# Windowed attention and a routed two-layer MLP on one core: second weights loaded by expert and only when missing, and the small tiled matmuls of a unit issued in one block

## Chip, cores, metric

The kernel runs on one core of a Trainium2 chip. The metric is the device time of one execution in microseconds (us). Executions of one kernel scatter by about 1% either way here, so kernels are compared by runs that were interleaved on one chip: a ratio below is the mean time of one kernel's fast runs over the mean of the other's fast runs of the same rounds, so it is not quite the ratio of the medians that stand beside it. A run is called slow when it is over 1.5% above the fastest run of the same kernel; slow runs are left out of the ratios.

## The reference, cut to what matters

```python
# attention: 8 batches x 8 heads, 576 positions, head size 64, causal window of 64
scores = scale * q @ k.T, masked to 0 <= i - j < 64
x = softmax(scores) @ v                       # -> (8, 576, 512), heads side by side
# one expert of 8 per batch
e = argmax(mean(x, axis=1) @ w_gate)          # per batch
out = softmax_weight * (relu(x @ w1[e]) @ w2[e])   # w1: 512x1024, w2: 1024x512
```

With the fixed inputs, the experts of the eight batches are 5 4 2 7 1 5 7 2: five different ones, and the last three batches repeat earlier ones.

## The kernel before

A batch is worked in five slots: four head pairs and one slot for the last 64 positions. In slot `s` the kernel does the values step of unit `s-1` (`st_a`, PSUM tile `av`, normalised by DVE into `x`), the scores of unit `s` (`st_s`, tile `sp`), the transposes of q and k for unit `s+2` (`tr`, tile `tp`, 8 and 10 of them), and the transposes of `x` of unit `s-2` (`st_x`, tile `xps`). `fill(part)` puts expert work of an earlier batch in between: first matmuls (`ph`, 4 matmuls a chunk) and second matmuls (`po`, 8 a chunk). The values, scores and q/k transposes use half of the PE array each (tiled modes); expert matmuls and most transposes of `x` use all of it.

```python
wp  = tc.tile_pool(name="wp", bufs=3)      # expert weights w1t, w2t
op_ = tc.tile_pool(name="op", bufs=4)      # output tiles ob
ps  = tc.tile_pool(name="ps", bufs=6, space=PSUM)   # av, tp, xps, ph, po, gl, glp in turn
...
def norm(u, av, n, x):                     # frees an av buffer
    nc.vector.reciprocal(out=rl, in_=avv[:, :, D:D + 1])
    nc.vector.tensor_tensor(out=x, in0=avv[:, :, 0:D], in1=rl, op=ALU.mult)
...
def gate(b):
    # gl = pooled @ w_gate on PE; then gs, gm (max), gi (index) on DVE
    nc.gpsimd.load(ereg, gi[0:1, 0:1])                       # index into a register
    nc.gpsimd.dma_start(out=w1t, in_=w1e[esl].squeeze(0))    # 2 MB read, 1 MB written as fp16
    nc.gpsimd.dma_start(out=w2t, in_=w2e[esl].squeeze(0))
    # nm, ge (exp on ACT), gr
...
for s in range(NSLOT + 4):
    st_a(s - 1, 0); st_a(s - 1, 1)
    fill(0.1)
    mask_it = st_s(s)
    fill(0.3)
    tr(n, 0)
    mask_it()
    fill(0.5)
    st_x(s - 2)
    fill(0.75)
    tr(n, 1)
    cast_v(n); load_qk(n + 5); load_v(n + 3)
    fill(1.0)
    if s >= 7 and (s - 7) % NU == 0: gate((s - 7) // NU)
    if s >= 8 and (s - 8) % NU == 0: gate2((s - 8) // NU)
# then the expert work that is left
```

The softmax here doesn't subtract the row's maximum and nothing guards it: scores larger than these inputs give would overflow.

## Time and profile before

| kernel before | |
|---|---|
| median of the first 6 runs | 247.73 us (246.2 to 249.53) |
| profiled span | 246.9 us |
| start until the first expert matmul | 51.9 us |
| one batch in the middle (five slots) | 26.10 us |
| last batch's first expert matmul to the end | 21.2 us |

The page's slices of the kernel before; each digit is the busy share of one fortieth of the span, in tenths, and PEclk is the granted TensorE clock:

```profile
PE   0458876659999999999999999999999999998992
PEclk9999996559999999999999999999999999999999
DMA  6999999999499999999999999994993099479723
```

From 51.9 us on PE is idle only once, for 0.73 us, before its last matmuls are done. (The clock record begins only at 32.5 us here, and before its first entry the views print full clock. That is no measurement: in after_again, below, it begins at 55.1 us, and the first expert matmuls before that start 0.24 us apart, those after it 0.12 us. So the start ran at half clock there too.) The windows view gives the busy time of each engine between the starts of successive batches' first expert matmuls (third column: PE; the DMA share adds up the times of packets that overlap, so it can exceed 1):

```profile
core 0: us, PE busy (x) PEld busy (x) DVE busy (x) ACT busy (x) POOL busy (x), PEclk, DMA share, GB/s
79.93:106.03 26.10, 26.10 (x355) 15.92 (x351) 19.32 (x56) 15.20 (x38) 12.61 (x23) 1.00 1.11 219
184.33:207.09 22.76, 22.76 (x270) 13.85 (x266) 15.20 (x46) 11.68 (x30) 1.49 (x2) 1.00 0.58 122
207.09:225.69 18.60, 17.87 (x121) 10.55 (x118) 6.86 (x18) 6.15 (x17) 1.48 (x2) 1.00 0.75 155
225.69:246.87 21.18, 16.77 (x104) 10.12 (x104) 6.32 (x10) 4.94 (x12) 0.00 (x0) 1.00 0.52 141
```

PE is busy for all of the 26.10 us, so a gain there must come out of PE's own time. The timeline of PE in the middle shows where some of it is lost (start, duration of the merged group, line, tile; matmuls overlap, so the start-to-start difference is the cost):

```profile
113.56 1.16 PE L286 MATMUL ph<-xT,w1t 128*128 128x288 f16 x8
114.55 0.39 PE L228 MATMUL xps<-ident,x 128*128 128x128 f16 x4
114.77 0.65 PE L286 MATMUL ph<-xT,w1t 128*128 128x288 f16 x4
115.36 0.47 PE L147 MATMUL tp<-ident,qk 128*64 128x128 f16 x10
115.76 1.16 PE L286 MATMUL ph<-xT,w1t 128*128 128x288 f16 x8
116.84 0.35 PE L243 MATMUL gl<-wg,pl 128*1 128x8 f32 x8
```

Eight expert matmuls followed by the same mode (`128*128`) take 0.99 us, followed by another mode 1.08: about 0.1 us at each change. There are some 15 such changes out of expert work in a batch.

Last, the end: the last gate's matmul, its w1 load, and the first matmul that needs it. PE waits only 0.73 us for the load, since it still has the second matmuls of the batch before to do:

```profile
214.36 0.35 PE L243 MATMUL gl<-wg,pl 128*1 128x8 f32 x8
216.34 0.74 POOL L259 DMA_DIRECT2D w1t<-in_moe_w_dram  x1 [17.12 <-DVE gr L267]
225.69 0.54 PE L286 MATMUL ph<-xT,w1t 128*128 128x288 f16 x3 [0.73 <-DMA w1t<-in_moe_w_dram]
```

### The profile page before, as it was taken

What the parts mean: (1) busy time and instruction counts of PE and PEld (TensorE: products, weight loads), DVE (VectorE), ACT (ScalarE), POOL (GpSimd) and SP (SyncE); (2) the same over time, 40 slices, a digit from 0 to 9 for tenths busy, and PEclk for the clock granted to TensorE, in tenths of its full rate; (3) what the DMA queues carried; (4) which work ended last, traced back from release to release, by engine and by line L of the source; (5) the groups of instructions that cost most, each with busy time, mean ns of one, the idle gap of its engine ahead of it and who ended that gap; (6) DMA issues with size and microseconds to landing.
All of it is one profiled execution on the core that took longest, in us unless ns stands there. A gap on an engine that the chain in (4) does not pass through costs nothing.

```text
span 246.9 us, 7106 instructions
## 1 busy us (share of the span) xinstructions
PE 218.8 (89%) x2800; PEld 137.1 (56%) x2800; DVE 158.4 (64%) x460; ACT 125.2 (51%) x289; POOL 106.0 (43%) x191
## 2 busy tenths in 40 slices
PE   0458876659999999999999999999999999998992
PEld 0346555436655675566556665666556755745741
DVE  3467898807677767787768776886777564343232
ACT  2256667526734774377527753666357723602500
POOL 7987998942293139424772459022800110020000
PEclk9999996559999999999999999999999999999999
DMA  6999999999499999999999999994993099479723
GB/s 126 197 212 193 202 186 197 175 205 202 92 160 223 198 302 162 215 200 302 167 210 202 286 179 196 209 292 95 178 255 102 4 165 259 110 111 243 181 94 97
DMA packets 61489, 45.57 MB, mean 185 GB/s; under 512 B 40464, under 2 KB 48656, under 8 KB 61456
## 3 DMA queue, kind: packets, MB, share of 16 engines
q0 software_dynamic: 17664, 26.22, 62.7%
q1 hardware_dynamic: 43792, 18.90, 32.1%
q8 instruction: 22, 0.36, 0.6%
q14 instruction: 11, 0.09, 0.1%
HBM read 61.88 MB, written 9.44 MB: 289 GB/s over the span
## 4 chain that ended last, share of the span: by engine, by line
PE 73%; DMA 13%; POOL 6%; SPq 3%; issue 3%; DVE 1%; POOLq 0%; ACT 0%
PE ph L286 29%; PE po L301 25%; DMA w1t<-in_moe_w_dram 8%; PE tp L147 6%; DMA v_126<-in_v_dram 5%; PE sp L167 4%; PE av L202 3%; PE xps L228 3%; SPq L76 2%; POOL qk L65 2%; PE av L211 1%; PE gl L243 1%; PE glp L272 1%; POOL vx_149 L133 1%; POOL vxt_161 L137 0%
## 5 line engine op out<-in xcount | busy, mean ns | idle before, releaser
L286 PE MATMUL ph<-xT,w1t 128*128 128x288 f16 x512 | 77.1, 291 | 4.6 <-DMA w1t<-in_moe_w_dram 4.6
L301 PE MATMUL po<-w2t,hT 128*128 128x512 f16 (+1 forms) x320 | 74.9, 380 | 0.0
L286 PEld LDWEIGHTS <-w1t 128*128 128x128 f16 x512 | 44.9, 99 | 18.9 <-DMA w1t<-in_moe_w_dram 5.2
L174 ACT ACTIVATE pt<-sp 128x1024 f16<-128x1024 f32 (+1 forms) x40 | 37.6, 939 | 27.3 <-PE sp L167 27.0
L305 DVE TENSOR_SCALAR ob<-po,gw 128x512 f32<-128x512 f32 (+1 forms) x40 | 30.0, 749 | 30.3 <-PE po L301 27.7
L291 ACT ACTIVATE hT<-ph 128x288 f16<-128x288 f32 x96 | 37.6, 413 | 21.7 <-PE ph L286 20.0
L301 PEld LDWEIGHTS <-hT 128*128 128x128 f16 (+1 forms) x320 | 29.9, 100 | 31.1 <-issue 0.8
L147 PE MATMUL tp<-ident,qk 128*64 128x128 f16 x576 | 32.0, 249 | 10.7 <-DMA qk<-in_k_dram 10.7
L186 DVE TENSOR_TENSOR x<-av,rl 128x256 f16<-128x256 f32 (+1 forms) x80 | 33.8, 423 | 2.7
L147 PEld LDWEIGHTS <-qk 128*64 128x64 f16 x576 | 21.2, 125 | 20.6 <-issue 15.6
L259 POOL DMA_DIRECT2D w1t<-in_moe_w_dram x8 | 6.0, 755 | 56.4 <-DVE rl L185 38.8
L230 ACT ACTIVATE xT<-xps 128x512 f16<-128x512 f16 x32 | 19.2, 601 | 19.3 <-PE xps L228 19.3
L65 POOL DMA_DIRECT2D qk<-in_q_dram x32 | 19.7, 614 | 20.2 <-PE av L202 12.6
L177 DVE TENSOR_TENSOR pt<-pt,mask 128x1024 f16<-128x1024 f16 (+1 forms) x40 | 25.5, 637 | 0.7 <-ACT pt L174 0.6
L293 DVE TENSOR_SCALAR hT<-ph 128x288 f16<-128x288 f32 x32 | 14.5, 452 | 14.0 <-PE ph L286 14.0
L65 POOL DMA_DIRECT2D qk<-in_k_dram x32 | 19.5, 608 | 0.0
L202 PEld LDWEIGHTS <-pt 128*64 128x64 f16 x512 | 12.1, 120 | 9.9 <-DVE pt L177 8.1
L228 PE MATMUL xps<-ident,x 128*128 128x128 f16 (+1 forms) x160 | 16.1, 227 | 0.0
L228 PEld LDWEIGHTS <-x 128*128 128x128 f16 (+1 forms) x160 | 10.8, 102 | 8.4 <-issue 3.6
L185 DVE RECIPROCAL rl<-av 128x4 f32<-128x4 f32 (+1 forms) x80 | 13.6, 170 | 1.1 <-PE av L211 1.0
L153 ACT COPY kT_131<-tp 128x256 f16<-128x256 f16 (+1 forms) x12 | 5.5, 456 | 9.2 <-DVE qT_133 L152 9.0
L152 DVE COPY qT_148<-tp 128x256 f16<-128x256 f16 (+1 forms) x10 | 4.6, 463 | 8.5 <-PE tp L147 8.5
(211 smaller groups left out, 225.8 us busy)
## 6 DMA issues: line engine op xcount, KB each, us to landing
w1t<-in_moe_w_dram POOLq DMA_DIRECT2D x8, 1024.0 KB, 8.8
w2t<-in_moe_w_dram POOLq DMA_DIRECT2D x8, 1024.0 KB, 15.1
out_dram<-ob SPq DMA_DIRECT2D x32, 256.0 KB, 7.8
qk<-in_q_dram POOLq DMA_DIRECT2D x32, 144.0 KB, 6.8
qk<-in_k_dram POOLq DMA_DIRECT2D x32, 144.0 KB, 7.0
out_dram<-ob SPq DMA_DIRECT2D x8, 128.0 KB, 7.1
v_99<-in_v_dram SPq DMA_DIRECT2D x2, 128.0 KB, 3.0
v_110<-in_v_dram SPq DMA_DIRECT2D x2, 128.0 KB, 6.7
```

The costliest lines, as they stand in the source:

```text
L65: nc.gpsimd.dma_start(out=t[64 * i:64 * i + 64].rearrange("p h t d -> p h (t d)"), in_=src[b, 2 * hp:2 * hp + 2, :, :].rearrange("h (p t) ...
L147: nc.tensor.transpose(out=tp[64 * hh:64 * hh + 64, t].rearrange("p a b -> p (a b)"), in_=qks[n][:, hh, lo + t, :], identity=ident)
L174: nc.scalar.activation(out=pv, in_=sp[:, :, 0:64 * m], func=AF.Exp, scale=scale)
L177: nc.vector.tensor_tensor(out=pv, in0=pv, in1=mk.unsqueeze(1).broadcast_to([128, 2, 64 * m]), op=ALU.mult)
L186: nc.vector.tensor_tensor(out=x.rearrange("p (g d) -> p g d", d=D), in0=avv[:, :, 0:D], in1=rl[0:n].broadcast_to([n, 4, D]), op=ALU.mult)
L202: nc.tensor.matmul(out=av[64 * jj:64 * jj + 64, o:o + D + 1], lhsT=pt[:, hh, 2 * i + jj, :], rhs=vx[:, 1 - jj, i, hh, :], start=True, stop ...
L228: nc.tensor.transpose(out=tp[:, g], in_=x[0:n, g, :], identity=ident[0:n, 0:n])
L230: nc.scalar.activation(out=xTs[b][:, c, 0:512], in_=tp.rearrange("p g t -> p (g t)"), func=AF.Copy, accum_out=pps[b][:, c:c + 1])
L286: nc.tensor.matmul(out=ph[:, 0:SC], lhsT=w1v[:, kb, ft // 2, ft % 2, :], rhs=xTs[b][:, kb, ts(sc, SC)], start=(kb == 0), stop=(kb == NHP - 1))
L291: nc.scalar.activation(out=dst, in_=ph[:, 0:SC], func=AF.Relu)
L301: nc.tensor.matmul(out=po[0:n], lhsT=st["h"][:, ft, 128 * i:128 * i + n], rhs=w2t[:, ft // 2, ft % 2, :], start=(ft == 0), stop=(ft == 7))
L305: nc.vector.tensor_scalar(out=ob[0:n], in0=po[0:n], scalar1=gws[b][0:n, 0:1], scalar2=None, op0=ALU.mult)
```

## The change

Two ideas. All eight experts' second weights get a place of their own in SBUF (`WT`), so that an expert that comes again need not be loaded again; DVE keeps a vector of experts already seen and POOL issues the w2 load under the condition that this one is new. The second matmuls then address `WT` through a register. And the three tiled steps of a slot are put next to each other, with two fills instead of five, so that PE changes its mode less often.

```diff
-    wp = ctx.enter_context(tc.tile_pool(name="wp", bufs=3))
+    wp = ctx.enter_context(tc.tile_pool(name="wp", bufs=2))
+    WT = const.tile([128, E, 8 * Dm], FP16)
 def gate(b):
+        nc.vector.tensor_copy(out=gf, in_=gi[:, 0:1])
+        nc.vector.tensor_scalar(out=oh, in0=iota, scalar1=gf, ..., op0=ALU.is_equal)
+        nc.vector.tensor_tensor(out=st2, in0=oh, in1=seen, op=ALU.mult)
+        nc.vector.tensor_tensor(out=seen, in0=seen, in1=oh, op=ALU.max)
+        nc.vector.reduce_sum(out=gf, in_=st2, axis=AX.X)
+        nc.vector.tensor_copy(out=ei[:, 0:1], in_=gi[:, 0:1])
+        nc.vector.tensor_copy(out=ei[:, 1:2], in_=gf)
-        nc.gpsimd.load(ereg, gi[0:1, 0:1])
+        nc.gpsimd.load(ereg, ei[0:1, 0:1])
+        nc.gpsimd.load(hreg, ei[0:1, 1:2])
         nc.gpsimd.dma_start(out=w1t, in_=w1e[...])
-        nc.gpsimd.dma_start(out=w2t, in_=w2e[...])
+        nc.gpsimd.dma_start(out=WT[expert e], in_=w2e[...], cond=have < 1)
 # h_chunk, first of a batch
+        nc.tensor.load(pe, eis[b][0:1, 0:1])
 # o_chunk
-        rhs=w2t[:, ft // 2, ft % 2, :]
+        rhs=WT[:, ds(st["e"], 1), :]...[:, ft, :]
 # slot
             st_a(s - 1, 0); st_a(s - 1, 1)
-            fill(0.1)
             mask_it = st_s(s)
-            fill(0.3)
             tr(n, 0)
+            tr(n, 1)
             mask_it()
-            fill(0.5)
+            fill(0.3)
             st_x(s - 2)
-            fill(0.75)
-            tr(n, 1)
             cast_v(n); ...
             fill(1.0)
# ... cut: dependency declarations, and three loads moved up in the prologue
```

More of the change, by code (lines that the diff above doesn't have):

```diff
@@ L15 @@
 AX = mybir.AxisListType
+SYNC = mybir.DependencyInfo(mybir.DependencyClass.Sync, mybir.DependencyReason.DATA)
 @with_exitstack
@@ L54 @@
     qks, v32s, v8s, xTs = {}, {}, {}, {}
-    pts, xs, wts, gws, pps = {}, {}, {}, {}, {}
+    pts, xs, wts, gws, pps, eis, w1s = {}, {}, {}, {}, {}, {}, {}
     NP = B * NHP
@@ L82, in load_v @@
             nc.sync.dma_start(out=t8[64:128], in_=v[b, :, 512:576, :].rearrange("h p d -> p h d"))
+    WT = const.tile([128, E, 8 * Dm], FP16)
+    loads, tmms = [], []
     ident = const.tile([128, 128], FP16)
@@ L100 @@
     load_v(2)
+    load_qk(3)
+    load_v(3)
+    load_qk(4)
     wg = const.tile([128, NHP, E], FP32)
     nc.sync.dma_start(out=wg, in_=moe_w_gate.rearrange("(kb p) e -> p kb e", p=128))
-    load_qk(3)
-    load_v(3)
+    iota = const.tile([1, E], FP32)
+    for e in range(E):
+        nc.vector.memset(iota[:, e:e + 1], float(e))
+    seen = const.tile([1, E], FP32)
+    nc.vector.memset(seen, 0.0)
     ones1 = const.tile([1, 128], FP32)
@@ L250, in gate @@
         nc.vector.max_index(out=gi, in_max=gm, in_values=gs)
-        ereg = nc.gpsimd.alloc_register(f"er{b}")
-        nc.gpsimd.load(ereg, gi[0:1, 0:1])
-        esl = ds(nc.gpsimd.snap(ereg, donate=True), 1)
-        w1t = wp.tile([128, NHP, F], FP16, tag="w1t", name="w1t")
-        w2t = wp.tile([128, 4, 2, Dm], FP16, tag="w2t", name="w2t")
-        wts[b] = (w1t, w2t)
+        gf = gp.tile([1, 1], FP32, tag="gf", name="gf")
+        nc.vector.tensor_copy(out=gf, in_=gi[:, 0:1])
+        oh = gp.tile([1, E], FP32, tag="oh", name="oh")
+        nc.vector.tensor_scalar(out=oh, in0=iota, scalar1=gf, scalar2=None, op0=ALU.is_equal)
+        st2 = gp.tile([1, E], FP32, tag="st2", name="st2")
+        nc.vector.tensor_tensor(out=st2, in0=oh, in1=seen, op=ALU.mult)
+        nc.vector.tensor_tensor(out=seen, in0=seen, in1=oh, op=ALU.max)
+        ei = gp.tile([1, 2], U32, tag="ei", name="ei", bufs=4)
+        nc.vector.reduce_sum(out=gf, in_=st2, axis=AX.X)
+        nc.vector.tensor_copy(out=ei[:, 0:1], in_=gi[:, 0:1])
+        nc.vector.tensor_copy(out=ei[:, 1:2], in_=gf)
+        eis[b] = ei
+        ereg = nc.gpsimd.alloc_register(f"er{b}")
+        nc.gpsimd.load(ereg, ei[0:1, 0:1])
+        hreg = nc.gpsimd.alloc_register(f"hr{b}")
+        nc.gpsimd.load(hreg, ei[0:1, 1:2])
+        e = nc.gpsimd.snap(ereg, donate=True, min_val=0, max_val=E - 1)
+        have = nc.gpsimd.snap(hreg, donate=True, min_val=0, max_val=1)
         w1e = moe_w1.rearrange("e (kb p) f -> e p kb f", p=128)
         w2e = moe_w2.rearrange("e (g p r) d -> e p g (r d)", p=128, r=2)
-        nc.gpsimd.dma_start(out=w1t, in_=w1e[esl].squeeze(0))
-        nc.gpsimd.dma_start(out=w2t.rearrange("p g r d -> p g (r d)"), in_=w2e[esl].squeeze(0))
+        w1t = wp.tile([128, NHP, F], FP16, tag="w1t", name="w1t")
+        w1s[b] = w1t
+        nc.gpsimd.dma_start(out=w1t, in_=w1e[ds(e, 1)].squeeze(0))
+        W2 = WT[:, ds(e, 1), :].squeeze(1).rearrange("p (g x) -> p g x", g=4)
+        mine = [nc.gpsimd.dma_start(out=W2, in_=w2e[ds(e, 1)].squeeze(0), cond=have < 1)]
+        for d in mine:
+            for other in tmms + loads:
+                tc.declare_no_dep(d.ins, other, reason="an expert is loaded before its first use")
+        loads.extend(d.ins.name for d in mine)
+        wts[b] = [d.ins.name for d in mine]
         nm = gp.tile([1, 1], FP32, tag="nm", name="nm")
@@ L278, in moe_chunks, with mm @@
         st = {}
+        def mm(**kw):
+            m = nc.tensor.matmul(**kw)
+            for d in loads:
+                if d not in wts[b]:
+                    tc.declare_no_dep(m.ins, d, reason="another expert, or loaded long before")
+            for d in wts[b]:
+                tc.add_manual_dep(m.ins, d, SYNC, reason="the weights of this expert")
+            tmms.append(m.ins.name)
         def h_chunk(ft, sc):
             if ft == 0 and sc == 0:
+                pe = nc.tensor.alloc_register(f"pe{b}")
+                nc.tensor.load(pe, eis[b][0:1, 0:1])
+                st["e"] = nc.tensor.snap(pe, donate=True, min_val=0, max_val=E - 1)
                 st["h"] = hp_.tile([128, 8, S], FP16, tag="hT", name="hT")
-            w1v = wts[b][0].rearrange("p kb (g x r) -> p kb g r x", r=2, x=128)
+            w1v = w1s[b].rearrange("p kb (g x r) -> p kb g r x", r=2, x=128)
             ph = ps.tile([128, 512], FP32, tag="b", name="ph")
@@ L298, in o_chunk @@
             po = ps.tile([128, 512], FP32, tag="b", name="po")
-            w2t = wts[b][1]
+            w2t = WT[:, ds(st["e"], 1), :].squeeze(1).rearrange("p (f d) -> p f d", d=Dm)
             for ft in range(8):
-                nc.tensor.matmul(out=po[0:n], lhsT=st["h"][:, ft, 128 * i:128 * i + n],
-                                 rhs=w2t[:, ft // 2, ft % 2, :],
+                mm(out=po[0:n], lhsT=st["h"][:, ft, 128 * i:128 * i + n],
+                                 rhs=w2t[:, ft, :],
                                  start=(ft == 0), stop=(ft == 7))
@@ L319 @@
     with tc.manual_schedule():
-        load_qk(4)
         tr(0, 0)
@@ L341, in fill @@
                     spent += cost
+            n = NHP * b + c + 2 if c < NHP else NP
             if 0 <= s - 1 < NSLOT:
@@ L345 @@
                 st_a(s - 1, 1)
-            fill(0.1)
             mask_it = st_s(s) if s < NSLOT else None
-            fill(0.3)
-            n = NHP * b + c + 2 if c < NHP else NP
             tr(n, 0)
+            tr(n, 1)
             if mask_it:
                 mask_it()
-            fill(0.5)
+            fill(0.3)
             if 0 <= s - 2 < NSLOT:
                 st_x(s - 2)
-            fill(0.75)
-            tr(n, 1)
             cast_v(n)
```

## The prediction

> **What bounds the kernel now.** (1) 0 to 52 us: loads. The page's slices show DMA at 90% or more from the second slice; the chain of waits runs through v loads, POOL and 11.5 us of the first w1t load; PE waits 3.8 us for it, at half clock. (2) 52 to 207 us: PE. The windows view shows it without idle time; the timeline repeats every 26.10 us (five slots, one batch). (3) 207 to 247 us: the last batch. The last gate's w1t load starts at 216.3 and lands at 225.6, PE waits 0.7 us, then 21 us of expert matmuls and stores.
>
> **What the change removes.**
> - Array mode switches. In the steady timeline 8 expert matmuls (L286) followed by the same mode cost 0.98 us, followed by a tiled block 1.09: 0.11 us of drain. The Trainium skill, "TensorEngine Tiling (Array Packing)", Key Properties, says that changing the tiling mode drains the TensorE; the trace agrees (weight loads idle 0.24 us at each switch). About 15 excursions per 26.1 us become about 6: 9 x 0.11 = 1.0 us. Eight q/k transposes take 0.34 us alone, 0.25 right behind the scores (3 a period, 0.27); the ten others 0.41 alone, estimated 0.30 behind the eight (4 a period, 0.4). Estimate: 1.7 us per period.
> - Three w2 loads: by the reference the experts are 5 4 2 7 1 5 7 2, so the last three batches repeat. Those loads (172, 198, 217 us) come after q, k and v have landed and behind their own w1t, so they shorten nothing that PE waits for: about 0.
>
> **What it adds.**
> - Seven tiny DVE operations at the gate (0.12 to 0.2 us each by its timeline) and a second register load on POOL: w1t starts about 1.3 us later. Critical at the first batch (offset, because that slot's scores and transposes now run before the wait) and at the last: +1.3. Elsewhere w1t lands 5 us before use: free.
> - A register load on PE per batch, estimate 0.4 us from POOL's 0.5 of "issue".
> - Register-addressed second matmuls (320). POOL's address MOVE takes 29 ns; one or two per 216 ns matmul should hide. Unsure.
> - w1 in two buffers: its last reader is done two slots earlier; free.
>
> **Limit.** By the DMA packet records, fewer than 14 packets are in flight in only 5% of the steady period: DMA is about 95% used. A period of 24.8 us meets that floor. q and k land 20 us before use, v about 5, so a small shortfall is absorbed.
>
> **Sum.** (1.7 - 0.4) x about 5.5 periods = -7; start 0 +/- 1; tail +1.3; floor +0.5. 247.7 - 5.3 = 242.3 us (rounded), range 238 to 246.5. Faster by over 2%: 0.52; within 2%: 0.41; slower: 0.07.
>
> **What would show it.** Steady period 24.6 to 25.2 us, PE still without idle time; 6 tiled excursions per period; q/k transposes in one group of 18 of 0.55 us; second matmuls still 1.73 us per 8; last w1t about 1.3 us later after its gate; w2t bytes down by three loads of 1 MB with no time gained.
>
> **What would make it wrong.** Register addressing slowing matmuls or stopping the weight prefetch (50 ns each costs 16 us); PE idle at the block's seams because transposes, exp, copies and PSUM buffers come in bursts (ACT estimate 4.8 us per 5 us slot in the first-matmul stage); DMA falling behind, with waits on v or w1t; a longer half-clock start.

## More of the kernel before

The gate's operations on DVE, and what DVE does next, the normalisation of the next slot (`x`):

```profile
117.69 0.15 DVE L250 FIND_INDEX8 gi<-gm,gs 1x8 uint32<-1x8 f32 x1
117.76 0.12 DVE L262 TENSOR_SCALAR nm<-gm 1x1 f32<-1x1 f32 x1
...
118.61 0.42 DVE L186 TENSOR_TENSOR x<-av,rl 128x256 f16<-128x256 f32 x1
```

## The result, and the profile after

| | median | ratio to before (95% interval) |
|---|---|---|
| before (20 runs) | 248.37 us (246.11 to 249.77) | |
| after (10 runs) | 253.22 us (251.45 to 258.62) | 1.0183 (1.0139 to 1.0227) |

The changed kernel is slower by 1.8%, where 2.2% faster was predicted. Its time lies outside the stated range.

Its first profile fell on a slow run (256.1 us). Some of the changed kernel's runs take 256 to 258.6 us, the rest 251.5 to 253.6. So it was run and profiled again, unedited, to get a fast one of 251.1 us (run "after_again" below), and the lines here are of that one. The windows view, again from batch to batch; the names are those of the lines before:

```profile
79.21:105.22 26.01, 25.12 (x355) 16.59 (x351) 19.77 (x63) 14.95 (x37) 12.34 (x24) 1.00 1.10 221
184.36:206.93 22.57, 21.55 (x234) 13.52 (x231) 15.58 (x51) 11.11 (x29) 0.75 (x2) 1.00 0.46 98
206.93:228.31 21.38, 18.04 (x119) 10.63 (x118) 7.70 (x25) 5.46 (x15) 0.74 (x2) 1.00 0.50 110
228.31:251.10 22.79, 18.42 (x104) 10.85 (x103) 5.58 (x9) 4.92 (x12) 0.00 (x0) 0.89 0.16 57
```

A batch in the middle takes 26.01 us against 26.10: nearly nothing was gained. But PE is now idle for 0.89 us of it, which it never was before. The last two stages take 21.38 and 22.79 us against 18.60 and 21.18: 4.4 us lost at the end.

The seam in the middle. PE in the slot behind a gate, with the wait that PE had in brackets:

```profile
114.18 0.34 PE L252 MATMUL gl<-wg,pl 128*1 128x8 f32 x8
114.46 0.45 PE L211 MATMUL av<-vx,pt 128*64 128x65 f16 x16
114.84 0.41 PE L176 MATMUL sp<-qT,kT 64*128 64x64 f16 x16
115.17 0.69 PE L156 MATMUL tp<-ident,qk 128*64 128x128 f16 x18
115.80 1.16 PE L327 MATMUL ph<-xT,w1t 128*128 128x288 f16 x8
117.50 0.40 PE L237 MATMUL xps<-ident,x 128*128 128x128 f16 x4 [0.54 <-DVE x L195]
118.25 1.02 PE L310 MATMUL po<-WT,hT 128*128 x4 [0.36 <-DVE x L195]
```

The merge itself works: one block of 16 + 16 + 18 tiled matmuls stands where there were three or four excursions. But then PE waits twice for DVE's `x`. DVE at the same time:

```profile
115.02 0.15 DVE L259 FIND_INDEX8 gi<-gm,gs 1x8 uint32<-1x8 f32 x1
115.21 0.14 DVE L261 CAST gf<-gi 1x1 f32<-1x1 uint32 x1
...
116.09 0.14 DVE L270 CAST ei<-gf 1x1 uint32<-1x1 f32 x1
116.16 0.13 DVE L291 TENSOR_SCALAR nm<-gm 1x1 f32<-1x1 f32 x1
...
117.02 0.42 DVE L195 TENSOR_TENSOR x<-av,rl 128x256 f16<-128x256 f32 x1
...
117.56 0.42 DVE L195 TENSOR_TENSOR x<-av,rl 128x256 f16<-128x256 f32 x1
```

From the index to the first `x` it is now 2.00 us (115.02 to 117.02), before 0.92 (117.69 to 118.61). The normalisation frees the PSUM buffers of `av`. The block takes four of the six buffers (two `av`, two `tp`) and the two chunks of the first fill take the other two, so the seventh tile, `xps`, must wait for the first `av`, and the next one (`po`) for the second: the two waits above. (This is read from the order in the code and the named waits; no run changed the number of PSUM buffers.) The list of waits shows the two once per batch, five times each (columns: total us, times, longest), and the wait for w1 at the end:

```profile
PE ph L327 <- DMA w1t<-in_moe_w_dram: 3.3, 1, 3.3
...
PE xps L237 <- DVE x L195: 2.7, 5, 0.5
PE po L310 <- DVE x L195: 1.8, 5, 0.4
```

The end, from the last gate's matmul to the first matmul that needs its weights:

```profile
214.21 0.34 PE L252 MATMUL gl<-wg,pl 128*1 128x8 f32 x8
...
217.60 0.74 POOL L282 DMA_DIRECT2D w1t<-in_moe_w_dram  x1 [20.84 <-PE po L310]
...
227.98 0.10 PEld L327 LDWEIGHTS <-w1t 128*128 128x128 f16 x1 [3.48 <-DMA w1t<-in_moe_w_dram]
228.31 1.51 PE L327 MATMUL ph<-xT,w1t 128*128 128x288 f16 x9 [3.32 <-DMA w1t<-in_moe_w_dram]
```

From gate to load it takes 3.39 us (before 1.98), the load lands 10.3 us after its issue (before 9.3), and 0.33 us pass between the first weight load and the first matmul (before none); the trace has the register load on PE, 0.30 us, at the start of that stretch. PE is idle for 3.32 us instead of 0.73. And the clock drops: the last stage has a mean granted clock of 0.89, and the trace's clock record shows 3.41 us at half clock from 229.2 us on. The Trainium skill, "TensorE: Matmul & The Clock Gate", Part 1, says that the clock is halved after an idle window of about 3.4 us and that the window is 3413 ns long; this trace agrees with the length (3.41 us), but not with a whole window of idle time: on the grid of the clock record, the window before the half clock (225.77 to 229.18 us) was idle for 2.54 us only.

In the slow run the half clock near the end lasts 6.83 us instead of 3.41, and there is one more wait, at 161 us, in DVE and then in PE:

```profile
160.56 0.74 DVE L346 TENSOR_SCALAR ob<-po,gw 64x512 f32<-64x512 f32 x1 [4.37 <-DMA out_dram<-ob]
161.35 0.85 PE L327 MATMUL ph<-xT,w1t 128*128 128x288 f16 x5 [3.36 <-DVE ob L346]
```

The fifth output tile of a batch needs the first one's `ob` buffer, and that one's store had not yet landed: issued at 147.06 us, it landed at 160.46.

### The profile page after: what moved, and what is told of

Read it like the earlier page. It is cut to its first block, busy times and chain, and to the rows that moved or that the text cites. A ratio compares the mean times of both kernels' runs of the same rounds, so it can differ in the third digit from the quotient of the medians.

```text
span 256.1 us, 7515 instructions
## 1 busy us (share of the span) xinstructions
PE 218.8 (85%) x2800; PEld 144.8 (57%) x2800; DVE 166.4 (65%) x525; ACT 124.0 (48%) x289; POOL 101.4 (40%) x191
## 4 chain that ended last, share of the span: by engine, by line
PE 60%; DMA 16%; DVE 14%; issue 4%; ACT 2%; POOL 2%; POOLq 0%; DVEq 0%; ACTq 0%
PE ph L327 24%; PE po L310 18%; DMA w1t<-in_moe_w_dram 8%; PE tp L156 6%; DMA out_dram<-ob 5%; PE sp L176 4%; PE av L211 4%; DVE pt L186 3%; DVE x L195 3%; DMA qk<-in_k_dram 3%; PE xps L237 2%; PE av L220 1%; POOL qk L66 1%; ACT ge L294 1%; DVE ob L346 1%
## 5 line engine op out<-in xcount | busy, mean ns | idle before, releaser
L327 PE MATMUL ph<-xT,w1t 128*128 128x288 f16 x512 | 73.3, 298 | 7.7 <-DMA w1t<-in_moe_w_dram 3.8
L310 PE MATMUL po<-WT,hT 128*128 (+1 forms) x320 | 73.3, 379 | 1.9 <-DVE x L195 1.8
L327 PEld LDWEIGHTS <-w1t 128*128 128x128 f16 x512 | 49.8, 102 | 24.1 <-issue 4.7
L310 PEld LDWEIGHTS <-hT 128*128 128x128 f16 (+1 forms) x320 | 31.0, 100 | 36.1 <-issue 2.8
L156 PE MATMUL tp<-ident,qk 128*64 128x128 f16 x576 | 27.9, 256 | 10.1 <-DMA qk<-in_k_dram 10.1
L156 PEld LDWEIGHTS <-qk 128*64 128x64 f16 x576 | 21.9, 132 | 12.3 <-issue 10.4
L186 DVE TENSOR_TENSOR pt<-pt,mask 128x1024 f16<-128x1024 f16 (+1 forms) x40 | 26.8, 669 | 0.1
L211 PEld LDWEIGHTS <-pt 128*64 128x64 f16 x512 | 12.7, 122 | 14.0 <-DVE pt L186 12.2
L237 PEld LDWEIGHTS <-x 128*128 128x128 f16 (+1 forms) x160 | 10.2, 104 | 8.4 <-DVE x L195 4.4
L244 DVE TENSOR_REDUCE pl<-xT 128x4 f32<-128x256 f16 x8 | 3.4, 419 | 9.3 <-ACT xT L242 9.3
```

The costliest lines, as they stand in the source:

```text
L156: nc.tensor.transpose(out=tp[64 * hh:64 * hh + 64, t].rearrange("p a b -> p (a b)"), in_=qks[n][:, hh, lo + t, :], identity=ident)
L186: nc.vector.tensor_tensor(out=pv, in0=pv, in1=mk.unsqueeze(1).broadcast_to([128, 2, 64 * m]), op=ALU.mult)
L211: nc.tensor.matmul(out=av[64 * jj:64 * jj + 64, o:o + D + 1], lhsT=pt[:, hh, 2 * i + jj, :], rhs=vx[:, 1 - jj, i, hh, :], start=True, stop ...
L237: nc.tensor.transpose(out=tp[:, g], in_=x[0:n, g, :], identity=ident[0:n, 0:n])
L310: m = nc.tensor.matmul(**kw)
L327: nc.tensor.matmul(out=ph[:, 0:SC], lhsT=w1v[:, kb, ft // 2, ft % 2, :], rhs=xTs[b][:, kb, ts(sc, SC)], start=(kb == 0), stop=(kb == NHP - 1))
```

## The experiments

Twelve runs in three sessions; each session interleaves its kernels with the kernel before on one chip. Medians of the kernel before were 249.0 us (the first four rows below), 248.86 (merge_ob8 to pool_ob8) and 247.85 (the last four).

| run | median us | ratio to before (95%) | one batch in the middle | last wait for w1 | last stage |
|---|---|---|---|---|---|
| after_again | 252.83 | 1.0218 (1.008 to 1.035) | 26.0 to 26.8 | 3.3 | 22.8 |
| merge_only | 248.6 | 1.0059 (0.996 to 1.016) | 24.8 to 31.8 | 0.8 | 21.2 |
| cond_only | 252.7 | 1.0200 (1.009 to 1.031) | 26.1 | 3.2 | 22.8 |
| gate_early | 248.02 | 0.9988 (0.986 to 1.012) | 25.5 to 31.3 | none | 21.1 |
| merge_ob8 | 239.23 | 0.9672 (0.962 to 0.973) | 24.8 to 25.2 | 0.7 | 21.2 |
| after_ob8 | 251.7 | 1.0136 (1.006 to 1.022) | 26.0 to 26.2 | 3.3 | 22.8 |
| cond_w1first | 248.0 | 0.9912 (0.980 to 1.002) | 26.1 | 1.8 | 21.1 |
| pool_ob8 | 241.26 | 0.9733 (0.967 to 0.980) | 24.9 to 25.2 | 1.8 | 21.2 |
| before_ob8 | 248.75 | 1.0028 (0.997 to 1.009) | 26.1 | 0.9 | 21.2 |
| after_w1first_ob8 | 245.77 | 0.9920 (0.987 to 0.997) | 25.9 to 26.1 | 1.6 | 21.1 |
| w1first_noskip | 247.9 | 0.9995 (0.993 to 1.006) | 26.1 | 1.4 | 21.2 |
| merge_ob8_gate_early | 239.63 | 0.9650 (0.959 to 0.971) | 24.9 | none | 21.2 |

The three right columns are in us and come from one profiled run each (those of gate_early and cond_w1first count as slow, the others as fast); "last stage" is from the last batch's first expert matmul to the end. All runs were correct.

### The changed kernel again

No edit.

> The changed kernel once more, unedited, for a trace in the fast state (the first one is in the slow state: 256.1 us, clock 0.978). Both theories: fast runs 251 to 253 us, ratio about 1.018. What is to be read: whether the 3.4 us PE stall on a store at 157 us and the half-clock stretch after the last w1t wait are there in the fast state too.

Measured: three fast runs (252.39 to 252.89 us) and one slow (257.64). The 3.4 us stall on a store is not in this fast trace (the largest wait for `ob` is 1.0 us), the wait for w1 and the half clock at the end are. So, in the two traces at hand, the slow run of this kernel is the one in which a store holds PE up.

### One half at a time

The merge alone: the slot of the changed kernel in the kernel before.

```diff
--- before
+            n = NHP * b + c + 2 if c < NHP else NP
-            fill(0.1)
             mask_it = st_s(s) if s < NSLOT else None
-            fill(0.3)
             tr(n, 0)
+            tr(n, 1)
             mask_it()
-            fill(0.5)
+            fill(0.3)
             st_x(s - 2)
-            fill(0.75)
-            tr(n, 1)
```

> The kernel before, with only the new order (tiled matmuls in one block, two fills). Theory G (the longer DVE chain of the gate stands in front of the normalisation at a seam without filler, and eats what the merge gains): the merge gains about 1.2 us per batch, most of it stays: period about 25.1 us, total 242 to 244, ratio 0.975 to 0.985. Rival R1 (the merge itself stalls on PSUM buffers and evictions and gains nothing): period 26 us, total 247 to 250, ratio 1.00 or above.

Measured: ratio 1.006, 248.6 us. By the total, the rival R1 looked right, and my theory G missed. But the trace shows neither: four of the batches take 24.8 to 26.4 us, and one takes 31.8, with this in it (DVE, then PE):

```profile
132.32 0.74 DVE L305 TENSOR_SCALAR ob<-po,gw 64x512 f32<-64x512 f32 x1 [5.32 <-DMA out_dram<-ob]
133.12 2.08 PE L286 MATMUL ph<-xT,w1t 128*128 128x288 f16 x8 [4.31 <-DVE ob L305]
```

The first store of that batch was issued at 117.88 us and landed at 132.23, and at 132.32 DVE went on. Around that idle time the clock record shows 6.8 us at half clock. All five runs had a mean clock of 0.982 or 0.983, so they all seem to have had this stall. The merge did gain in the middle, and the stores gave it back. This was a cause that I had not named.

The conditional loads alone: the changed kernel with the old slot (the reverse of the diff above; the loads moved up in the prologue stay).

> The changed kernel with the old order of the slot: only the conditional loads, with flags, register loads and register-addressed second matmuls. Theory G: the flag operations hide behind the fills in the middle, period 26.1 to 26.3 us, and only the last gate costs about 1.3 us: total 248.5 to 250, ratio 1.003 to 1.01. Rival R2 (register loads or register-addressed matmuls cost by themselves): period 26.8 or more, ratio 1.015 or more.

Measured: ratio 1.02, 252.7 us, which by the number alone is what R2 (registers cost by themselves) had expected. The windows view says otherwise:

```profile
105.25:131.35 26.10, 26.10 (x355) 15.91 (x351) 20.50 (x63) 15.01 (x38) 13.04 (x23) 1.00 1.11 218
...
207.67:228.96 21.29, 18.03 (x118) 10.63 (x118) 7.84 (x26) 5.58 (x15) 0.74 (x2) 1.00 0.48 105
228.96:251.80 22.84, 18.42 (x104) 10.85 (x103) 5.57 (x9) 4.93 (x12) 0.00 (x0) 0.89 0.17 62
```

The middle is 26.10 us, to the hundredth that of the kernel before: neither the flags nor the register loads nor the register-addressed matmuls (40 a batch) cost anything there. All the loss is at the end: the last two w1 loads start 3.3 us behind their gates instead of 2.0 and take 10.6 and 10.3 us instead of 8.8 and 9.3, PE waits 1.2 and 3.2 us, and then the clock halves. The last three stages lost 1.4, 2.7 and 1.7 us, not the 1.3 in all that G had put there.

### The gate moved away from the seam

```diff
+            if s >= 7 and (s - 7) % NU == 0: gate((s - 7) // NU)
             fill(1.0)
-            if s >= 7 and (s - 7) % NU == 0: gate((s - 7) // NU)
```

> The changed kernel with the gate emitted before the second fill of its slot instead of behind it, so that its DVE operations run while PE has expert work, not in front of the next normalisation. Theory G: the 1.3 us stall per batch behind the gate goes, period about 24.9 to 25.2 us, the last w1t also starts some us sooner: total 242 to 246, ratio 0.975 to 0.99. R1 or R2: the stall per batch stays or shows elsewhere, period 26 us, total above 248.

Measured: 248.0 us, 4.8 us below the changed kernel but above what was expected. The trace (a slow run, 248.3 us) shows two batches of 25.46 us, no wait for `x` behind a gate (some of 0.4 to 0.5 us for ACT in its place), and no wait for w1 at the end; but again one batch of 31.3 us with a PE wait of 3.4 us behind `ob`. So the wait behind the gate and the one at the end go away with the gate's place, as theory G has it, though the batch of 25.46 us is still above the 24.9 to 25.2 that G forecast; and the store stall is a thing of its own. Three of the four runs have a mean clock of 0.986, among them the traced one with its stall and 6.83 us at half clock; the fourth has 0.999 and took 244.83 us, within G's 242 to 246.

### More output buffers

```diff
-    op_ = ctx.enter_context(tc.tile_pool(name="op", bufs=4))
+    op_ = ctx.enter_context(tc.tile_pool(name="op", bufs=8))
```

In the merge alone:

> The merge alone with eight output buffers (ob) instead of four. In the merge-only trace undisturbed batches take 24.8 to 25.1 us, but PE stood still 4.3 us behind a DVE output scaling that waited for a store to leave one of the four ob buffers, and then ran at half clock for 6.8 us. Theory S (the merge gains 1.0 to 1.3 us per batch and the late stores give it back through the ob buffers): no such wait, all batches near 25 us, total 241 to 244, ratio 0.97 to 0.985. Rival D (the 16 DMA engines are simply full up to 165 us, so a faster PE must wait somewhere): the wait moves to v, q, k or w1t, batches average 26 us, total 246 to 249.

Measured: 239.2 us, ratio 0.967, better than theory S had it. The windows view:

```profile
51.34:76.51 25.17, 25.17 (x352) 16.65 (x351) 18.02 (x53) 14.88 (x37) 14.35 (x27) 1.00 1.16 212
76.51:101.32 24.81, 24.81 (x355) 16.51 (x351) 18.83 (x56) 14.94 (x37) 12.62 (x24) 1.00 1.13 218
101.32:126.40 25.08, 24.94 (x354) 16.50 (x350) 18.85 (x56) 15.02 (x37) 11.91 (x22) 1.00 1.13 223
```

Batches of 24.8 to 25.2 us with PE busy all but 0.14 us; from the second on that is 1.0 to 1.3 us less than before. The rival D, that the DMA engines are full and a faster PE must wait somewhere, falls for this speed: PE waits for no load in these batches. Stores take up to 17.5 us to land while loads are under way, and 2.0 us at the very end, when none are. They had taken up to 16.1 us in the kernel before as well, but those were second stores; its first stores, which the fifth output tile waits for, landed in 7.5 to 7.7 us in the first five batches. The merge did not shorten the time that they had: from the first store's issue to the end of the fifth tile's matmuls it is 9.11 us in the first five batches of either kernel. What changed is the landing: 14.35 us in the stall of merge_only, up to 17.5 in merge_ob8. There, v loads had been issued on the same queue (SP) shortly before the store and were still under way (in the stall those of 114.51 and 115.06 us, which landed at 126.04 and 130.84; the store landed at 132.23); in the kernel before, the next v loads followed the store. In all 14 traces, each first store of the first five batches that took more than 8.4 us had such v loads ahead of it. That they hold it up is what this suggests; no run moved them. The Trainium skill, "DMA: Bandwidth & Descriptors", "Issuing engines are not separate DMA queues", says that DMAs of all issuing engines run on the same 16 DMA engines and interleave; these landing times fit that but do not test it.

The control, the kernel before with eight buffers:

> Control: the kernel before with eight ob buffers and nothing else. Theory S: PE never waited for ob in its trace, so the buffers alone gain nothing: batches 26.1 us, ratio 0.995 to 1.005. If the buffers alone were the gain: ratio below 0.985.

Measured: ratio 1.003. The buffers alone gain nothing that these runs can show, nor does the merge alone (1.006, 0.996 to 1.016). Together they are worth 3.3%.

In the changed kernel:

> The changed kernel with eight ob buffers. Theory S: the 3.4 us stall of its slow runs goes, so most runs fall in the fast state, 250 to 251.5 us; batches still 26.0 us because of the 0.9 us DVE seam behind the gate, and the end still late (last w1t wait 3.3 us, then half clock): ratio 1.005 to 1.015. Rival D: slow runs of 256 to 258 us stay.

Measured: 251.7 us (expected: 250 to 251.5), ratio 1.014. None of the six runs reached 254 us (the largest is 253.3), where 4 of the 12 listed first runs of the changed kernel had been at 256 us or above. Batches are still 26.0 us and the end is still late, as expected.

### The late w1 load taken away

The w1 load is issued from the gate's index at once, as in the kernel before; the flags follow on DVE after the gate's own operations. In the old slot order:

```diff
         nc.vector.max_index(out=gi, in_max=gm, in_values=gs)
+        nc.gpsimd.load(ereg, gi[0:1, 0:1])
+        nc.gpsimd.dma_start(out=w1t, in_=w1e[ds(e, 1)].squeeze(0))
+        # nm, ge, gr as before
         # the flags on DVE: gf, oh, st2, seen, ei
-        # load of ei[0], ei[1]; w1t
+        nc.gpsimd.load(hreg, ei[0:1, 0:1])
         # w2 under its condition
-        # nm, ge, gr
```

> The conditional loads in the old order, but the w1t load is issued straight from the gate's index as in the kernel before, and the flags are worked out on DVE afterwards. Theory T (the whole loss of the conditional loads is that the last two w1t loads start 1.3 us later, run into more store traffic, and leave PE idle long enough to lose its clock): gate to w1t 2.0 us as before, last w1t wait under 1 us, no half clock at the end, total 247 to 249, ratio 0.995 to 1.005. Rival R2 (skipped loads or register addresses cost by themselves): w1t still takes 10.3 to 10.6 us to land in the last three batches, total 250 or more.

Measured: gate to w1 2.0 us again; the last wait for w1 is 1.8 us (expected: under 1), the clock no longer halves at the end, and the last stage takes 21.1 us (all from the trace of a slow run, 248.9 us). The median is 248.0 us against 248.9. The ratio (0.991) rests on two fast runs only, because one run of 243.95 us made the others count as slow; I take from it no more than "about as before". Theory T holds for its main part: the loss of the conditional loads is the late load. About 1.1 us of the last wait stayed.

The same with the condition removed, so that w2 is always loaded:

```diff
-        mine = [nc.gpsimd.dma_start(out=W2, in_=w2e[ds(e, 1)].squeeze(0), cond=have < 1)]
+        mine = [nc.gpsimd.dma_start(out=W2, in_=w2e[ds(e, 1)].squeeze(0))]
```

> The conditional loads in the old order with w1t first, but the condition taken off: w2 is loaded for every batch, also for repeated experts. If the skip saves time: the total rises above that of the same kernel with the skip (248.0 us). My theory: the skip saves nothing, total within 0.5% of it. In its last two batches w1t took 9.8 and 10.0 us to land with the skip, 8.8 and 9.3 in the kernel before: if the skip itself slows w1t, that goes back to 8.8 and 9.3 here.

Measured: 247.9 us with all eight loads against 248.0 with five. The two ran in different sessions; as ratios to the kernel before they are 0.9995 (0.993 to 1.006) and 0.991 (0.980 to 1.002, two fast runs), and the intervals overlap. Skipping three loads of 2 MB saved no time that these runs can show. The last two w1 loads took 9.1 and 9.5 us here, 9.8 and 10.0 with the skip. Two further traces with the skip and the early w1 load show the same: 10.1 and 9.8 (after_w1first_ob8), 10.5 and 10.0 (pool_ob8). So the skip may even slow the w1 load beside it by half a microsecond, but I have no cause for it: open.

In the merged order, with eight buffers:

> The changed kernel (merged order) with eight ob buffers and w1t issued straight from the gate's index, the flags worked out on DVE after the gate's own operations. It splits the two roles of the flags: the late w1t is gone, the seven operations still stand on DVE in front of the normalisation. Theory: the 0.9 us PE seam behind each gate stays, batches 25.9 to 26.1 us, the end is as in the kernel before within 1.2 us: total 246.5 to 248.5, ratio 0.99 to 1.0. If the seam came from the late w1t: batches 25 us, total 241.

Measured: 245.8 us, ratio 0.992. The end is nearly as before (last wait 1.6 us, clock 1.0), the seam is still there:

```profile
115.73 0.40 PE L237 MATMUL xps<-ident,x 128*128 128x128 f16 x4 [0.41 <-DVE x L195]
116.49 1.24 PE L309 MATMUL po<-WT,hT 128*128 x5 [0.36 <-DVE x L195]
```

PE is idle for 0.77 us behind each gate (the flags are six operations here, one copy fewer), batches 25.9 to 26.1 us. That separates the two roles of the flag operations. Between the trace of the changed kernel with eight buffers (249.7 us) and this one (243.4 us), 5.0 of the 6.3 us lie in the last three stages.

### The flags on POOL

```diff
-        nc.vector.tensor_copy(out=gf, in_=gi[:, 0:1])        # ... seven operations on DVE
+        # w1t issued from gi first, then on POOL:
+        nc.gpsimd.tensor_copy(out=gf, in_=gi[:, 0:1])
+        nc.gpsimd.tensor_scalar(out=oh, in0=iota, scalar1=gf, ..., op0=ALU.is_equal)
+        nc.gpsimd.tensor_tensor(out=st2, in0=oh, in1=seen, op=ALU.mult)
+        nc.gpsimd.tensor_tensor(out=seen, in0=seen, in1=oh, op=ALU.add)
+        # three adds for the sum, a cast, the register load, the conditional w2 load
```

> The changed kernel with w1t issued straight from the gate's index, the flags worked out on POOL instead of DVE, and eight ob buffers: the causes of T, S and the DVE seam taken away together. If these three are all: batches 25 us, end as in the kernel before, total 241 to 244, ratio 0.97 to 0.985. If something else costs: above 246.

Measured: 241.3 us, ratio 0.973; batches of 24.9 to 25.2 us and no wait behind the gates. PE goes from the first fill straight to the transposes (1.00 us for eight matmuls, where it had been 1.70):

```profile
113.03 1.16 PE L329 MATMUL ph<-xT,w1t 128*128 128x288 f16 x8
114.03 0.39 PE L237 MATMUL xps<-ident,x 128*128 128x128 f16 x4
```

With the late load, the seam and the store stall removed, the changed kernel beats the kernel before by 2.7%. So these three were what it lost, up to a rest: in the same session the merge with eight buffers and without conditional loads took 239.2 us, 2.0 less. 1.2 us of that is the last wait for w1, which is still 1.8 us here, not 0.7.

### A version that beats both

The merge with eight buffers and the gate ahead of the second fill:

> A version to beat the merge with eight ob buffers (239.2 us): the gate of a batch emitted before the second fill of its slot. The last w1t starts about 1.7 us sooner after PE's work allows, so the last w1t wait (0.66 us) goes; the middle is PE-bound and stays at 24.8 to 25.1 us per batch. Total 238 to 239.5, ratio 0.96 to 0.968. If DVE work of the gate now disturbs the fills: 240 or more.

Measured: 239.6 us, ratio 0.965; batches of 24.9 us and no PE wait of 0.25 us or more after the first expert matmul. The last wait for w1 is gone as expected, but the total can't be told from merge_ob8 (0.967 with an interval of 0.962 to 0.973). Either is 8 to 10 us faster than the kernel before, without any conditional load.

## Why the prediction was wrong, point by point

- **The gain of the merge: right in size, as far as PE's own time goes.** "Estimate: 1.7 us per period" was somewhat high; 1.0 to 1.3 us were measured (merge_ob8). The 18 transposes in one group cost 0.63 us, not 0.55, so that a slot saves about 0.12 us on them (0.34 and 0.41 apart). The Trainium skill, "TensorEngine Tiling (Array Packing)", Key Properties, which says that a change of tiling mode drains the TensorE, fits: about 0.1 us per change. How the gain divides between changes and transposes was not measured apart.
- **The step that failed first: "Elsewhere w1t lands 5 us before use: free."** I looked at the seven DVE operations only as a delay of the w1 load. They are also in front of the normalisation on DVE's queue, and the merge had just taken away the fill that hid this. In each batch PE is idle for 0.9 us (0.77 when the load goes first) and the batch takes 26.0 us instead of 24.8 to 25.2. So the term "(1.7 - 0.4) x about 5.5 periods = -7" came out near 0. Shown by pool_ob8 (flags on POOL: gone), after_w1first_ob8 (flags on DVE, load on time: stays), and cond_only (flags on DVE, old fills: 26.10, hidden).
- **The second: the end, "+1.3".** It measured about 4.4: 2.8 us in the last but one stage and 1.6 in the last. Of the 2.8, 1.4 is the later issue, 1.0 the slower landing of that load, 0.3 the register load on PE, which is exposed there; the 1.6 is the half clock that followed a wait of 3.3 us and did not follow one of 1.8 us (cond_w1first, pool_ob8). Why the load lands slower is not settled; part of it goes with the skip, part with the delay.
- **The third: "DMA falling behind, with waits on v or w1t."** The right worry in the wrong place, and it is what the slow runs and merge_only lost. v and w1 kept up in the middle; stores landing late held the `ob` buffers. I had listed the slack of the loads and never that of the stores: 9.11 us for the first store of a batch, which took up to 14.35 (merge_only). "A period of 24.8 us meets that floor" was not put to the test: batches came down to 24.81 us, and at that PE waited for no load once there were buffers. Whether the floor lies there or lower, no run shows.
- **"A register load on PE per batch, estimate 0.4 us": wrong in the middle.** It hides (cond_only: 26.10 us), and shows only where PE is waiting anyway, at the last w1 load.
- **Register-addressed second matmuls: right.** They cost nothing that the 26.10 us of cond_only shows.
- **The skipped loads: right, about 0.** 248.0 us with the skip, 247.9 without, in different sessions.
- The list of what would make it wrong named the idle seams and the half clock. I had given them too little weight: 0.07 for slower.

## What to carry to other kernels

Before taking out a fill between two steps, ask which short operations of other engines it was hiding, count how many buffers the longer block holds at once, and read the queue of the engine that frees them. A new order in the slot also moves the transfers against each other: here the first store kept its 9.11 us, but took longer to land when loads had been issued ahead of it. So check the output buffers as well as the prefetch; here a change of four buffers to eight was the difference between 0.6% slower and 3.3% faster. And a small delay at the end of a kernel can cost more than itself when it leads to an idle time long enough to lose the clock: here the 2.8 us lost ahead of the last batch brought 1.6 us at half clock with them.

## What the Trainium skill lacked or had wrong

- "TensorEngine Tiling (Array Packing)": says that changing the mode drains the TensorE, but gives no figure. Here about 0.1 us per change out of 128x128 work (0.99 against 1.08 us for eight matmuls).
- "TensorE: Matmul & The Clock Gate": "after ≥1 idle window (~3.4µs)". By the traces (PE idle time in the windows of 3.41 us that the clock records give, matmul ends being modelled) no window before a half clock was idle throughout: after 2.54 us in after_again and 1.93 us in gate_early the clock fell, after 1.84 us in cond_w1first it did not. One wait can cost two windows: 6.83 us at half clock in merge_only around a wait of 4.31 us. The 17.07 us in the kernel before (five windows) began at 39.3 us, in the loading stage and before the first w1 wait, after a window with only 1.47 us of idle time; so idle time alone does not tell when the clock falls.
- No page that I found gives the cost of loading a register from SBUF on an engine; "DMA: Bandwidth & Descriptors" has a `tensor_load` floor of about 600 ns and does not say from which memory. In after_again the TENSOR_LOAD instructions of POOL and PE took 0.29 to 0.31 us for the most part, 0.49 at most. On PE 0.33 us passed between weight load and matmul where the register load was exposed (227.98 to 228.31), and none showed in the middle.
- No page that I found gives the cost of matmuls addressed through a register or of a DMA issued under a condition. The matmuls left the batch at 26.10 us (cond_only); three skipped loads of 2 MB changed the total by nothing that the runs can show, their issue took POOL 0.04 to 0.05 us instead of 0.75 (after_again), and the w1 load issued just before a skipped one took 9.8 and 10.0 us against 9.1 and 9.5.
